# Grouping the attention score products on TensorE two rounds at a time, in a fused attention and MLP kernel

## The chip, the cores and the metric

The kernel runs on one core of a Trainium2 chip. The metric is the device time of one execution in microseconds: the median over three runs before the change is 751.19 us, and the change is judged by the same measurement.

## The reference

One input x of 2048 rows by 512 goes through two branches, which a gate mixes. Branch A is attention with 32 heads of 16 columns, where each row attends to itself and the 255 rows before it. Branch B is an MLP with 1792 hidden columns and a GELU.

```python
qkv = (x @ wqkv).reshape(B, S, 3, H, Dh).transpose(2, 0, 3, 1, 4)
q, k, v = qkv[0], qkv[1], qkv[2]
scores = einsum("bhqd,bhkd->bhqk", q, k) * Dh ** -0.5
mask = (i - j >= 0) & (i - j < 256)
o = einsum("bhqk,bhkd->bhqd", softmax(where(mask, scores, -1e9)), v)
a = o.transpose(0, 2, 1, 3).reshape(B, S, D) @ wo
b = gelu(x @ w1 + b1) @ w2 + b2
g = sigmoid((x * gate_w).sum(-1))
out = g * a + (1 - g) * b
```

## The kernel before

All dense products (x times wqkv, w1, w2, wo) are done with each operand split into a high and a low part, so one logical product is three matmuls of 128x512, on lines 108, 109 and 110 (`mm3`). One such step is called a dense step below; the Python generator `dense()` yields after each. It goes first through the query, key and value products (tiles `qk`, `v`), then through eight MLP passes (for each a stretch of seven tiles `u` with the GELU, and a stretch of four tiles `y`), and at last through the output product (tiles `a`).

Attention runs beside this. It works in eight groups of four heads, and each group in sixteen blocks of 128 rows, so there are 128 block steps. The scores are computed twice. The first time, `att_max` (a matmul on line 519 into a tile `sm`) puts 128x320 scores into PSUM, and VectorE reduces them to a maximum per row (line 524, tiles `jm` and `M`). The maxima of four blocks are turned round (`att_rows`, lines 536 to 546) and appended as rows to the queries. The second time, `att_exp` (a matmul on line 564 into a tile `st`) gives scores with the maximum already taken off, ScalarE writes their exponentials (line 586, tile `pt`), and GpSimd cuts the masked corners (line 580). After every fourth block, `att_pvs` multiplies 12 half blocks of exponentials with the values (line 608): many small matmuls into one bank of the `sm` ring and one of the `st` ring. ScalarE copies the one (line 629, tile `nd`), VectorE adds the other (line 632), and both banks are free again.

The PSUM rings are short: three buffers `sm`, three buffers `st`, two buffers `d` for the dense tiles. A product into `sm` can start when the product three places before it in that ring has been reduced; for `st`, when the third before it has been exponentiated. A bank that `att_pvs` takes counts as a place.

The order of instructions on each engine is fixed when the program is built. Python code issues the TensorE instructions in the order written, keeps a clock of estimated time (`tick`), and puts everything that follows a product on a heap with a delay (`after(ns, fn)`); what has come due is issued as the clock moves on. On the chip each engine executes its own list in order and waits for the others by semaphores.

The order around the change is set by the main loop, with `LEAD = 12`, `STEP = 2330`, `PVAT = 2` and `ORDER = 'mspf'`. Each block step u consists of four rounds i. A round issues one product of maxima (letter m, for the block 12 steps ahead), one product of exponentials (letter s), in round 2 the value products of the block before where they are due (letter p), and then a share of dense work (letter f). In the first twelve block steps there are only maxima, in the last twelve only exponentials.

```python
def fill(ns):
    owed[0] += ns
    while owed[0] > 0:
        c = next(run)          # one dense step; c is its estimate, 681
        ...
            owed[0] -= c
            tick(c)
```

A round owes 2330/4 = 582.5 of dense work and a dense step counts 3 x 227 = 681, so most rounds issue one dense step and about every seventh none.

Of the kernel before, what the change touches and what calls it, by code (L numbers as in the profile page):

```python
# [32 lines left out]
def gated_mix(ctx: ExitStack, tc: tile.TileContext, x, wqkv, wo, w1, b1, w2, b2, gate_w, out):  # L33
# [60 lines left out]
    for s in (0, 1):  # L94
        for k in (0, 1):
            v = own[64 * s:64 * s + 4].rearrange("r (p s) -> r s p", s=2)[:, s]
            nc.gpsimd.affine_select(out=v, in_=v, pattern=[[-2, 2]], compare_op=ALU.not_equal,
                                    fill=1.0, base=-k, channel_multiplier=1)
# [16 lines left out]
    def after(ns, fn, *args):  # L115
        now[1] += 1
        heapq.heappush(todo, (now[0] + ns, now[1], fn, args))
# [7 lines left out]
    def tick(ns):  # L125
        now[0] += ns
        while todo and todo[0][0] <= now[0]:
            step_todo()
# [331 lines left out]
    def load_ks(g_, c):  # L460


        ready(c, g_, 1)
        n = 2 * NB
        put_pairs([f32(ks[64 * s + 4:64 * s + 52, slot(g_, c)]) for s in range(2)], SK[c], g_)
# [16 lines left out]
    def load_kd(g_, c):  # L482
        for t in range(max(c - 1, 0), c + 1):
            ready(t, g_, 1)
            k0 = 0 if t == c else T - W
            at = W if t == c else 0
            src = heads(SK[t], g_)[:, :, :, :, k0:].rearrange("s d u a c -> (s d u) a c")
            nc.sync.dma_start(f32(kd[0:96, slot(g_, c), :, at:at + T - k0]), src)

    def load_qd(g_, c):  # L490
        ready(c, g_, 0)
        put_pairs([f32(qd[48 * s:48 * s + 48, slot(g_, c)]) for s in range(2)], SQ[c], g_)

    def load_qs(g_, c):
        ready(c, g_, 0)
        need(("v", NT - 2, NB - 1))
        for s in range(2):
            v = f32(qs[64 * s + 4:64 * s + 52, :, c * T:(c + 1) * T])
            nc.sync.dma_start(v, part(SQ[c], g_, s).rearrange("r (a c) -> r a c", a=2))

    def att_load_v(g_, c):
        need(*[("v", c, b) for b in range(NB)])
        vt = vbuf[:, c % 2]
        dst = vt[:, 0:NB * 68].rearrange("p (j c) -> p j c", c=34)
        nc.sync.dma_start(dst, SV[c].rearrange("p j s c -> p (j s) c")[:, :, 34 * g_:34 * g_ + 34])
        vts[g_, c] = vt

    def att_max(g_, b, i):

        if b % RB == 0 and (g_, b // RB) not in Ms:  # L510
            Ms[g_, b // RB] = sb.tile([128, 2 * RB, 2], F32, tag="M", bufs=2, name=f"M{g_}_{b}")
        M = Ms[g_, b // RB]
        hb, pr = divmod(i, 2)
        c, n = b // NB, slot(g_, b // NB)
        j = 2 * (b % NB) + hb
        w = min(64 * (2 * b + hb + 1), W + 64)
        k1 = 64 * (j + 1) + W
        p = ps.tile([128, 320], F32, tag="sm", bufs=3, name=f"sm{g_}_{b}_{i}")
        nc.tensor.matmul(p[:, :w], qd[0:96, n, pr, 128 * j:128 * (j + 1)], kd[0:96, n, pr, k1 - w:k1],  # L519
                         start=True, stop=True)  # L520
        junk = cs.tile([128, 320], BF16, tag="jm", bufs=1, name=f"jm{g_}_{b}_{i}")

        def red():
            nc.vector.tensor_tensor_reduce(junk[:, :w], p[:, :w], mask[:, 320 - w:320], 1.0, -3e38,  # L524
                                           ALU.add, ALU.max, M[:, 2 * (b % RB) + hb, pr:pr + 1])
            done.add(("max", g_, b, i))
        tick(w / 2.4 + 13)
        after(100, red)
# [310 lines left out]
    def load_y(t):  # L839

        need(*[("y", 1, t, b) for b in range(NB)])
        for i in range(NB // 2):
            if t < 2:
                v = f32(qd[:, t, i]).rearrange("p (j f) -> p j f", j=2)
            else:
                v = f32(kd[:, i, :, 0:T])
            nc.sync.dma_start(v, YB[t].rearrange("(i j p) f -> i p j f", j=2, p=128)[i])
            for j in range(2):
                ybs[t * NB + 2 * i + j] = v[:, j]
# [56 lines left out]
# [4 lines that stand above are left out]
            c = next(run)  # L910
            if c is None:
                owed[0] = -1e9
            else:
                owed[0] -= c
                tick(c)
# [7 lines left out]
    for u in range(-LEAD, NU):  # L923
        m = u + LEAD
        gm, bm = divmod(m, NKB)
        step = STEP if u >= 0 else STEP0
        for i in range(4):
            if i == 1 and m % NB == 0 and NB <= m < NU - NB:
                load_kd(*divmod(m // NB + 1, NT)), load_qd(*divmod(m // NB + 1, NT))
            for op in ORDER:  # L930
                if op == "s" and u >= 0:
                    att_exp(u // NKB, u % NKB, i)
                if op == "m" and m < NU:
                    att_max(gm, bm, i ^ XOR)
                if op == "p" and i == PVAT and u >= 1:
                    att_pvs(u - 1)
                if op == "f":
                    fill(step / 4 / ORDER.count("f"))
        if m < NU and bm % RB == RB - 1:
            after(900, att_rows, gm, bm // RB)  # L940
        if m % NB == QAT % NB and QAT <= m < QAT + NKB:
            load_qs(0, (m - QAT) // NB)
        if u % NB == 0 and NB <= u < NU - NB:
            load_ks(*divmod(u // NB + 1, NT))
        if u % NB == 2 and NB < u < NU - 3 * NB:
            load_qs(*divmod(u // NB + 3, NT))
        if u % NB == 0 and u >= 0:
            att_load_v(*divmod(u // NB, NT))
        if u - NU + NKB in (9, 11, 13):
            load_y((u % NKB - 9) // 2)  # L950
# [23 lines left out]
ORDER = 'mspf'  # L974
# [36 lines left out]
```

## Time and profile before

| | |
|---|---|
| three runs | 751.12, 751.19, 751.46 us; median 751.19 us |
| profiled execution | 752.58 us, of which 750.6 us are its span from the first to the last instruction |
| busy in the span | PE (TensorE) 98%, its weight loads 81%, DVE (VectorE) 69%, ACT (ScalarE) 57%, POOL (GpSimd) 50% |
| score products | 512 on line 519 (from 119.9 to 653.8 us), 512 on line 564 (the exponentials on ScalarE run from 161.7 to 699.6 us) |

The ends of matmuls are modelled, and matmuls overlap in the pipeline, so the cost of a matmul on TensorE is read as the distance from its start to the next start, not as its duration. "F" below is one dense step (lines 108, 109, 110), "m" a product on line 519, "s" one on line 564, "P" the value products on line 608.

### The profile page before, as it was taken

To read this page: it belongs to the slowest core of one execution; us is meant where nothing else is said; L and a number is where in the kernel's file an instruction comes from. 1 tells how busy PE (TensorE), PEld (TensorE's weight loads), DVE (VectorE), ACT (ScalarE), POOL (GpSimd) and SP (SyncE) were. 2 spreads that over 40 slices of the span, in tenths; PEclk is the share of its full clock that TensorE was granted. 3 is DMA by queue.
4 is the path that set the end of the run, shared out by engine and by line. 5 is a ranking of instruction groups with operands and counts; after the bars stand their busy time and mean duration, and the time that the engine had idled before them with its cause. 6 is when DMAs were issued, how large, how long until landed. Compare 5 with 4: busy or idle time off the path is not lost.

```text
span 750.6 us, 17969 instructions
## 1 busy us (share of the span) xinstructions
PE 733.8 (98%) x6129; PEld 605.3 (81%) x6129; DVE 519.6 (69%) x1567; ACT 430.9 (57%) x972; POOL 372.0 (50%) x846
## 2 busy tenths in 40 slices
PE   8999999998999999999999999999999999999998
PEld 6888888876788888888887877888888888878787
DVE  4532325789758867986898689868867886784552
ACT  4434522358547845864696478547845854785541
POOL 4200000339756765786577657757865875630000
PEclk9999999999999999999999999999999999999999
DMA  9889798998995687799576889996799898538783
GB/s 315 328 275 402 258 387 274 254 316 186 272 253 141 153 242 203 186 226 263 143 180 167 214 230 219 253 243 153 179 259 246 203 237 217 135 88 263 226 265 115
DMA packets 179258, 172.10 MB, mean 229 GB/s; under 512 B 56672, under 2 KB 122976, under 8 KB 179168
## 3 DMA queue, kind: packets, MB, share of 16 engines
q1 hardware_dynamic: 179168, 170.97, 81.0%
q8 instruction: 48, 0.79, 0.5%
q14 instruction: 42, 0.34, 0.2%
HBM read 108.53 MB, written 62.39 MB: 228 GB/s over the span
## 4 chain that ended last, share of the span: by engine, by line
PE 83%; DMA 6%; DVE 4%; ACT 2%; issue 2%; SPq 1%; POOL 0%; DVEq 0%; ACTq 0%; POOLq 0%
PE sm L519 9%; PE st L564 8%; PE y L108 7%; PE pv_sm L608 6%; PE y L110 6%; PE y L109 6%; PE u L108 5%; PE u L109 5%; PE u L110 5%; PE qk L110 4%; PE qk L108 4%; PE qk L109 4%; PE v L108 2%; PE a L108 2%; PE v L110 2%
## 5 line engine op out<-in xcount | busy, mean ns | idle before, releaser
L524 DVE CUSTOM_DVE_ANT_0 jm<-sm,mask 128x320 bf16<-128x320 f32 (+4 forms) x512 | 237.9, 465 | 83.4 <-PE sm L519 55.7
L580 POOL TENSOR_SCALAR_AFFINE_SELECT pt<-pt 64x256 f32<-64x256 f32 (+1 forms) x538 | 225.8, 440 | 118.6 <-ACT pt L586 108.2
L586 ACT ACTIVATE pt<-st 128x320 f32<-128x320 f32 (+4 forms) x512 | 207.1, 425 | 131.7 <-PE st L564 128.4
L519 PE MATMUL sm<-kd,qd 96*128 96x320 f32 (+4 forms) x512 | 156.3, 308 | 6.1 <-DVE M L524 3.8
L564 PE MATMUL st<-qs,ks 128*128 128x320 f32 (+4 forms) x512 | 155.7, 307 | 1.2 <-ACT pt L586 1.2
L546 POOL CAST qs<-tt 4x256 fp32r<-4x256 f32 x256 | 126.2, 493 | 42.4 <-DVE tt L539 31.4
L519 PEld LDWEIGHTS sm<-kd,qd 96*128 96x128 f32 x512 | 96.1, 188 | 34.3 <-DVE M L524 10.9
L564 PEld LDWEIGHTS st<-qs,ks 128*128 128x128 f32 x512 | 97.2, 190 | 21.5 <-ACT pt L586 2.3
L108 PE MATMUL y<-w,h 128*128 128x512 f32 x224 | 89.9, 401 | 0.0
L110 PE MATMUL y<-w,h 128*128 128x512 f32 x224 | 88.4, 395 | 0.3 <-DVE h L737 0.3
L109 PE MATMUL y<-w,h 128*128 128x512 f32 x224 | 88.2, 394 | 0.0
L108 PE MATMUL u<-mx,w 128*128 128x512 f32 x196 | 80.0, 408 | 0.0
L109 PE MATMUL u<-mx,w 128*128 128x512 f32 x196 | 77.3, 394 | 0.0
L110 PE MATMUL u<-mx,w 128*128 128x512 f32 x196 | 77.2, 394 | 0.0
L608 PE MATMUL pv_st<-pt,vbuf 64*32 64x320 f32 (+4 forms) x1408 | 73.2, 346 | 2.5 <-DVE pt L574 1.3
L608 PE MATMUL pv_sm<-pt,vbuf 64*32 64x320 f32 (+4 forms) x1408 | 74.1, 346 | 0.1
L608 PEld LDWEIGHTS pv_sm<-pt,vbuf 64*32 64x32 f32 x1408 | 51.1, 106 | 19.1 <-issue 2.3
L325 DVE TENSOR_TENSOR qke<-qk,qke 128x512 fp32r<-128x512 f32 x32 | 22.1, 690 | 47.4 <-ACT qke L322 39.3
L322 ACT ACTIVATE qke<-qk 128x512 fp32r<-128x512 f32 x32 | 19.1, 598 | 55.6 <-PE qk L110 32.3
L110 PEld LDWEIGHTS y<-w,h 128*128 128x128 f32 x224 | 42.1, 188 | 10.7 <-DVE h L737 1.2
L608 PEld LDWEIGHTS pv_st<-pt,vbuf 64*32 64x32 f32 x1408 | 46.0, 106 | 2.8 <-DVE pt L574 1.5
L338 POOL MEMSET vx<- 128x32 f32 x16 | 2.4, 156 | 89.2 <-DMA SQ<-qke 42.9
(148 smaller groups left out, 1334.4 us busy)
## 6 DMA issues: line engine op xcount, KB each, us to landing
kd<-SK SPq DMA_DIRECT2D x32, 384.0 KB
qs<-SQ SPq DMA_DIRECT2D x64, 192.0 KB
mx<-XT SPq DMA_DIRECT2D x24, 512.0 KB
SQ<-qke SPq DMA_DIRECT2D x16, 512.0 KB
SK<-qke SPq DMA_DIRECT2D x16, 512.0 KB
ND<-nd SPq DMA_DIRECT2D x32, 256.0 KB
raw_w<-in_B_w_dram SPq DMA_DIRECT2D x28, 256.0 KB
ks<-SK SPq DMA_DIRECT2D x32, 192.0 KB
```

Source lines behind the costliest of these rows:

```text
L108: nc.tensor.matmul(p, lh, rh, start=first, stop=False)
L109: nc.tensor.matmul(p, lh, rl, start=False, stop=False)
L110: nc.tensor.matmul(p, ll, rh, start=False, stop=last)
L322: nc.scalar.activation(e[:, h], p, AF.Copy)
L325: nc.vector.tensor_sub(e[:, 1 - h], p, f32(e[:, h]))
L519: nc.tensor.matmul(p[:, :w], qd[0:96, n, pr, 128 * j:128 * (j + 1)], kd[0:96, n, pr, k1 - w:k1], start=True, stop=True)
L524: nc.vector.tensor_tensor_reduce(junk[:, :w], p[:, :w], mask[:, 320 - w:320], 1.0, -3e38, ALU.add, ALU.max, M[:, 2 * (b % RB) + hb, pr:pr ...
L546: nc.gpsimd.tensor_copy(dst, src.unsqueeze(1).broadcast_to([4, 2, RB, 32]))
L564: nc.tensor.matmul(p[:, :w], ks[:, slot(g_, kb // NB), pr, at:at + 128], qs[:, pr, k0:k0 + w], start=True, stop=True)
L580: nc.gpsimd.affine_select(out=v, in_=v, pattern=[[0, v.shape[1]], [1 - 2 * e, 64]], compare_op=ALU.is_ge, fill=0.0, base=-e, channel_multi ...
L586: nc.scalar.activation(pt[:, hf, pr, :w], p[:, :w], AF.Exp, scale=SCALE)
L608: nc.tensor.matmul(pv[r // 64][32 * i:32 * i + 32, q - c * T:e - c * T], vts[g_, b // NB][r:r + 64, v:v + 32], rhs(r), start=start, stop=s ...
```

## The change

The loop over the four rounds now works on two rounds at a time. For rounds 0 and 1, and again for rounds 2 and 3, it issues the m, the s (and P, if due) of both rounds first, and then the two shares of dense work. So a row of m s F m s F becomes m s m s F F. Where a round owed no dense step, a pair has one F in place of two. In the first twelve block steps m F m F becomes m m F F, and in the last twelve s F s F becomes s s F F. The value products still follow the m and s of round 2, and now the m and s of round 3 follow them directly. The loads of `kd` and `qd` at `i == 1` are now issued after the dense work of rounds 0 and 1, not after that of round 0 alone. Nothing is added or removed.

```diff
         for i in range(4):
             if i == 1 and m % NB == 0 and NB <= m < NU - NB:
                 load_kd(*divmod(m // NB + 1, NT)), load_qd(*divmod(m // NB + 1, NT))
-            for op in ORDER:
+            if i % 2 == 0:
+                pair = (i, i + 1) if True else (i,)
+            elif len(pair) == 2:
+                continue
+            else:
+                pair = (i,)
+            for op, i in [(op, k) for k in pair for op in ORDER[:3]] + [("f", k) for k in pair]:
                 if op == "s" and u >= 0:
                     att_exp(u // NKB, u % NKB, i)
                 if op == "m" and m < NU:
@@
                 if op == "p" and i == PVAT and u >= 1:
                     att_pvs(u - 1)
                 if op == "f":
-                    fill(step / 4 / ORDER.count("f"))
+                    fill(step / 4)
```

On TensorE, at the end of the third set of value products (`pv_2`; its last matmul starts at 220.04 us in the profile), the order before is:

```order
L608 MATMUL pv_2_sm<-pt_6_2202,vbuf 32x128
L519 MATMUL sm_8_2_2659<-kd,qd 128x320
L564 MATMUL st_12_3_2663<-qs,ks 128x320
L108 MATMUL y_03_2530<-w_5_2001,h_5_2021 128x512
L109 MATMUL y_03_2530<-w_5_2001,h_5_2021 128x512
L110 MATMUL y_03_2530<-w_5_2001,h_5_2021 128x512
L519 MATMUL sm_9_1_2680<-kd,qd 128x320
L564 MATMUL st_13_0_2684<-qs,ks 128x320
L108 MATMUL y_03_2530<-w_6_2119,h_6_2144 128x512
L109 MATMUL y_03_2530<-w_6_2119,h_6_2144 128x512
L110 MATMUL y_03_2530<-w_6_2119,h_6_2144 128x512
L519 MATMUL sm_9_0_2693<-kd,qd 128x320
```

The same place on TensorE after the change (`sm_9_0` is the product of maxima for block 9, round 0, and so on; the last number is a buffer's):

```order
L608 MATMUL pv_2_sm<-pt_6_2202,vbuf 32x128
L519 MATMUL sm_8_2_2659<-kd,qd 128x320
L564 MATMUL st_12_3_2663<-qs,ks 128x320
L108 MATMUL y_03_2535<-w_5_2000,h_5_2032 128x512
L109 MATMUL y_03_2535<-w_5_2000,h_5_2032 128x512
L110 MATMUL y_03_2535<-w_5_2000,h_5_2032 128x512
L519 MATMUL sm_9_1_2680<-kd,qd 128x320
L564 MATMUL st_13_0_2684<-qs,ks 128x320
L519 MATMUL sm_9_0_2688<-kd,qd 128x320
L564 MATMUL st_13_1_2692<-qs,ks 128x320
L108 MATMUL y_03_2535<-w_6_2125,h_6_2152 128x512
L109 MATMUL y_03_2535<-w_6_2125,h_6_2152 128x512
```

`sm_9_0` takes the bank that `pv_2` gives back (the third place before it in the ring), and it now stands one dense step earlier behind the value products.

On VectorE, around the addition that frees the bank of the next set (`nd_3`), the order before is:

```order
L737 TENSOR_TENSOR h_0_3874<-x1h_0_3874_3882,h_0_3874 128x512
L650 RECIPROCAL den_0_3928<-den_0_3928 128x32
L731 SCALAR_TENSOR_TENSOR x1h_1_3948_3954<-sqh_1_3948_3955,x1h_1_3948_3954 128x512
L632 TENSOR_TENSOR nd_3_4044<-nd_3_4044,pv_3_sm 128x512
L524 ISA jm_12_2_4053,M_12_3939<-sm_12_2_4051,mask 128x320
L524 ISA M_12_3939 128x1
L524 ISA jm_13_1_4074,M_12_3939<-sm_13_1_4072,mask 128x320
```

and after the change it is:

```order
L737 TENSOR_TENSOR h_0_3878<-x1h_0_3878_3883,h_0_3878 128x512
L650 RECIPROCAL den_0_3928<-den_0_3928 128x32
L524 ISA jm_12_2_4047,M_12_3939<-sm_12_2_4045,mask 128x320
L524 ISA M_12_3939 128x1
L632 TENSOR_TENSOR nd_3_4044<-nd_3_4044,pv_3_sm 128x512
L731 SCALAR_TENSOR_TENSOR x1h_1_3955_3961<-sqh_1_3955_3962,x1h_1_3955_3961 128x512
L524 ISA jm_13_1_4074,M_12_3939<-sm_13_1_4072,mask 128x320
```

The reduction of the product that follows the value products has moved ahead of the addition on line 632, and a step of the GELU (line 731) has moved behind it.

## The prediction

> **What bounds the kernel now.** I read the page first, for the engine that is full.
>
> ```profile
> span 750.6 us, 17969 instructions
> PE 733.8 (98%) x6129; PEld 605.3 (81%) x6129; DVE 519.6 (69%) x1567; ACT 430.9 (57%) x972; POOL 372.0 (50%) x846
> PEclk9999999999999999999999999999999999999999
> ```
>
> TensorE is at work nearly all the time at full granted clock. The change adds and removes no matmul, so it can act in two ways only: the matmuls could follow each other more or less closely, and TensorE could wait more or less for a PSUM bank. For the second I looked at who holds up the products of maxima (the view of line 519), and who holds up VectorE (the view of waits).
>
> ```profile
> L519 PE MATMUL sm<-kd,qd x512: 193/311/418, 119.9 to 653.8; 96*128 96x320 f32 x150, 96*128 96x128 f32 x6, 96*128 96x64 f32 x5, 96*128 96x256 f32 x5
>   DVE M L524: 14.7, 32
>   DVE yo L811: 2.7, 2
>   DVE nd L632: 2.7, 4
> ```
>
> ```profile
> DVE nd L632 <- ACT nd L629: 23.2, 15, 3.0
> ```
>
> Of 512 products, 32 were held up by an earlier reduction, 14.7 us in all with their weight loads (which partly overlap other matmuls, so the loss is a little less), 2 by the end of a dense tile and 4 by the addition that frees the bank of the value products. Those are the waits to watch. Then the table of stretches, to see where they lie: busy times of PE, PEld, DVE, ACT and POOL in each.
>
> ```profile
> 170.00:180.00 10.00, 8.40 (x39) 5.93 (x38) 9.14 (x24) 8.59 (x20) 9.47 (x15) 1.00 0.68 157
> 180.00:190.00 10.00, 9.70 (x112) 7.82 (x111) 9.37 (x29) 8.86 (x20) 9.40 (x19) 1.00 1.08 274
> 300.00:320.00 20.00, 20.00 (x250) 16.53 (x249) 19.00 (x57) 16.04 (x35) 15.61 (x30) 1.00 0.77 191
> 340.00:360.00 20.00, 20.00 (x188) 16.86 (x187) 12.72 (x47) 8.89 (x21) 12.05 (x34) 1.00 0.89 254
> 380.00:400.00 20.00, 19.08 (x160) 15.88 (x159) 18.70 (x57) 17.36 (x39) 15.83 (x31) 1.00 0.81 181
> 440.00:450.00 10.00, 9.43 (x46) 7.28 (x46) 9.13 (x27) 8.33 (x19) 5.74 (x13) 1.00 0.88 208
> 450.00:460.00 10.00, 9.39 (x107) 7.07 (x105) 9.27 (x28) 8.92 (x19) 7.25 (x15) 1.00 0.97 222
> 460.00:470.00 10.00, 9.35 (x47) 7.47 (x46) 9.28 (x29) 8.20 (x20) 8.21 (x16) 1.00 0.88 219
> ```
>
> VectorE's mean of 69% hides two kinds of stage. In a `y` stage such as 340 to 360 it is busy 12.72 of 20 us and TensorE never waits. In a `u` stage, where the GELU steps come on top of the reductions, it is busy over nine tenths, and TensorE falls below full in six of the rows above (all but 300 to 320 and 340 to 360). There VectorE sets the pace, and how far TensorE may run ahead of it is a matter of the three `sm` banks.
>
> **The distance between matmuls.** Groups of four exist already, where a round owed no dense step. The timeline of TensorE shows one:
>
> ```profile
> 305.89 0.31 PE L519 MATMUL sm<-kd,qd 96*128 96x320 f32 x1
> 306.04 0.31 PE L564 MATMUL st<-qs,ks 128*128 128x320 f32 x1
> 306.19 0.32 PE L519 MATMUL sm<-kd,qd 96*128 96x320 f32 x1
> 306.34 0.31 PE L564 MATMUL st<-qs,ks 128*128 128x320 f32 x1
> 306.50 0.40 PE L108 MATMUL u<-mx,w 128*128 128x512 f32 x1
> ```
>
> Each score product takes 0.15 us (0.16 before the dense one), in a group of four as in a group of two, so regrouping costs TensorE nothing by itself. I take 0.0 us. Even 0.01 us for each of 256 groups would be 2.6 us in either direction, and I keep 1 us of that for the range.
>
> **The run-ahead.** A dense step takes 0.69 us, read from this place behind the value products `pv_2` (timeline of PE, ACT and DVE):
>
> ```profile
> 220.04 0.27 PE L608 MATMUL pv_sm<-pt,vbuf 64*32 64x128 f32 x1
> 220.24 0.42 PE L519 MATMUL sm<-kd,qd 96*128 96x320 f32 x1
> 220.40 0.60 ACT L629 ACTIVATE nd<-pv_st 128x512 f32<-128x512 f32 x1 [1.94 <-PE pv_sm L608]
> 220.49 0.31 PE L564 MATMUL st<-qs,ks 128*128 128x320 f32 x1
> 220.64 0.39 PE L108 MATMUL y<-w,h 128*128 128x512 f32 x1
> 220.69 0.49 DVE L524 CUSTOM_DVE_ANT_0 jm<-sm,mask 128x320 bf16<-128x320 f32 x1 [2.31 <-PE sm L519]
> 221.10 0.68 DVE L632 TENSOR_TENSOR nd<-nd,pv_sm 128x512 f32<-128x512 f32 x1
> 221.33 0.31 PE L519 MATMUL sm<-kd,qd 96*128 96x320 f32 x1
> 221.48 0.31 PE L564 MATMUL st<-qs,ks 128*128 128x320 f32 x1
> 221.63 0.39 PE L108 MATMUL y<-w,h 128*128 128x512 f32 x1
> 222.33 0.31 PE L519 MATMUL sm<-kd,qd 96*128 96x320 f32 x1
> ```
>
> The dense step runs from 220.64 to 221.33, 0.69 us, and a round with one lasts 0.99 to 1.00 us. A product of maxima reuses the bank of the third before it. Before, these two always lie three rounds apart: 3 x 0.99 = 2.97 us when every round has its dense step. After, it depends on the place in the pair. From the first m of a pair to the second m of the next pair lie two dense steps and six score products, 2 x 0.69 + 6 x 0.15 = 2.28 us; from the second m to the first m of the pair after the next, 3.66 us. The half that got more room gains nothing where there was enough. The half that got less is the one that counts: the reduction must now be over 0.69 us sooner. (Where a round owes no dense step, both figures are 0.69 us lower: 2.28 before, 1.59 after.)
>
> Where is a reduction later than 2.28 us? In the `u` stages. Two places from the timeline, each a product and what releases its bank; the first also with the product that waits for it:
>
> ```profile
> 173.48 0.34 PE L519 MATMUL sm<-kd,qd 96*128 96x320 f32 x1
> ...
> 176.75 0.48 DVE L524 CUSTOM_DVE_ANT_0 jm<-sm,mask 128x320 bf16<-128x320 f32 x1
> 177.16 0.08 DVE L524 DVE_READ_ACCUMULATOR2_ANT M<- 128x1 f32 x1
> 177.29 0.41 PE L519 MATMUL sm<-kd,qd 96*128 96x320 f32 x1 [0.65 <-DVE M L524]
> ...
> 447.45 0.31 PE L519 MATMUL sm<-kd,qd 96*128 96x320 f32 x1
> ...
> 449.44 0.49 DVE L524 CUSTOM_DVE_ANT_0 jm<-sm,mask 128x320 bf16<-128x320 f32 x1
> ```
>
> The product of 173.48 was reduced at 177.23, 3.75 us later. The product three places on would have been ready at 173.48 + 2.97 = 176.45 and waited until 177.29. The product of 447.45 was reduced at 449.93, 2.48 us later: no wait before, but 0.20 us beyond the new limit. So in stages where TensorE waits already, it arrives 0.69 us sooner at the same wait, and the backlog that it may build up is smaller by that. The loss comes once in each stretch, since afterwards VectorE sets the pace in both orders. I count one for each of the six rows in which PE is below full: 6 x 0.69 = 4.1 us. The lower bound is 0, if VectorE's order gets better by as much. The upper bound lets the shorter limit bite at every one of the 32 + 2 + 4 = 38 waits, one product in two being the tight one: 38 x 0.69 / 2 = 13.1 us.
>
> **The bank of the value products.** By the orders shown, the second m of the next pair takes this bank. Counted in the row of TensorE, after 7 of the 28 sets that have maxima behind them there is one dense step up to that m, after the others two. In the rows above, after the change: m at 220.24, s at 220.49, dense step 220.64 to 221.33, m at 221.33, s at 221.48, m due at 221.63. The addition on line 632 ends at 221.78, and a product follows its release by 0.05 us (177.24 to 177.29), so it starts at 221.83: 0.20 us lost. Before, the same product came at 222.33 and was safe. With two dense steps it comes 0.69 us later and is safe unless VectorE is behind. Seven times 0.20 is 1.4 us; two of the seven lie in `u` stages, where VectorE is later, and I add 0.45 us for each (two thirds of the addition's 0.68). Together 2.3 us, between 0 and 7 x 0.69 = 4.8 us.
>
> **What gets better.** The reduction of the m behind the value products moves ahead of the addition, while VectorE otherwise waits for ScalarE's copy: 23.2 us of waiting in 15 cases. This uses 0.48 + 0.08 = 0.56 us of idle time, but it is worth something only where VectorE is the bound: I count two sets in the slow stretches, 1.1 us gained, between 0 and 6 x 0.56 = 3.4 us. Exponentials have the same shorter distance on the `st` ring, but ScalarE is the lesser load in the rows above except near 450 to 460; I take 0 and leave this to the range. The loads of `kd` and `qd` start one half step later and are used four block steps later: 0.
>
> **The sum.** 0.0 + 4.1 + 2.3 - 1.1 = +5.3 us. The profiled execution, 752.6 us, would become 757.9; against the median of 751.2 this gives **756.5 us**.
>
> **Rivals.** *The waits go away (10%).* If the two reductions side by side and the earlier one behind the value products let VectorE run its list without holes, part of the 14.7 + 2.7 + 2.7 = 20.1 us would go; a third of it gives 751.2 - 6.7 = 744.5. It decides from the point where the holes filled outweigh 0.69 us a stretch. For it speak the 23.2 us of VectorE's waits, against it that VectorE is busy 9.1 to 9.4 of 10 us in those stretches and has few holes left.
>
> *Nothing moves (8%).* The rings suffice in the `y` stages, VectorE sets the pace in the `u` stages in either order, and only the seven sets cost: 751.2 + 1.4 - 1.1 = 751.5. Against it speaks that the limit of 2.28 us lies below lags that the trace shows.
>
> *The limit bites every time (13%).* With two dense steps in a row, VectorE runs dry during them and is overrun after them, so that the loss comes again in each pair: 751.2 + 13.1 + 2.3 = 766.6. Against it speaks that VectorE has three reductions queued when it is behind, 3 x 0.56 = 1.7 us of work, as long as the two dense steps.
>
> *The clock falls (1%).* In the stretches 170 to 190 and 380 to 400 TensorE has waits and a granted clock of 1.00 even at 8.40 of 10 us busy, so more of them should not change it. If it halved in the six waiting stretches, their PE time of 8.40 + 9.70 + 19.08 + 9.43 + 9.39 + 9.35 = 65 us would double, to 816 us. The Trainium skill, in "TensorE: Matmul & The Clock Gate", section "A second HAM failure mode: psum-queue depth-cycling", says that a kernel that cycles through PSUM banks can pause so often between matmul groups that the clock gate swings between half and full rate. By that rule this change would be the wrong direction; the trace, with short waits and 1.00 throughout, does not show it.
>
> **How the numbers follow.** The forecast, some microseconds slower, has 68%; its own range is 753 to 763. A measurement of this kernel can tell about 0.2%, 1.5 us, from no change. Faster by more than that is the first rival, 10%; within it the second, 8%; slower the rest, 82%. The range of 751.5 to 767 takes in the forecast, half of the second rival and nearly all of the third, and leaves out the first.
>
> **What would show it.** In the profile after, the waits of line 519 for M should grow from 32 cases to 40 or more, and those for nd from 4 to about 11. The stretches 170 to 190, 380 to 400 and 440 to 470 should show PE further below full, the `y` stages still full, and the score products should still start 0.15 us apart. The prediction is wrong if the waits shrink, if the products in a group of four spread to 0.19 us or more, or if TensorE waits in `y` stages beyond the seven places.

## The result, and the profile after

The kernel is slower by 3.0 us: 754.16 us (753.76 to 755.27 in six runs) against 751.15 us for the kernel before (749.35 to 751.54 in six runs), a ratio of 1.0040 with a 95% interval of 1.0026 to 1.0054. The forecast was +5.3 us, with a range that holds the result. The profiled execution has a span of 753.6 us, 3.0 more than before. The six executions of a kernel spread over 1.5 to 2.2 us here, and those of the kernel before over 4.9 to 7.2 us in the larger sets behind the experiments, so differences under one microsecond are read from many runs or not at all.

The page after, in the lines that answer to those of before:

```profile
span 753.6 us, 18000 instructions
PE 734.8 (98%) x6129; PEld 605.2 (80%) x6129; DVE 524.3 (70%) x1567; ACT 420.5 (56%) x972; POOL 372.7 (49%) x846
PEclk9999999999999999999999999999999999999999
```

The view of line 519 after, and then the one line of the view of line 564 that names ScalarE as the releaser, before and after:

```profile
  DVE M L524: 21.4, 43
  issue: 4.0, 20
...
  DVE nd L632: 0.2, 1
```

```profile
  ACT pt L586: 3.5, 8
```

```profile
  ACT pt L586: 7.1, 12
```

The products of maxima wait 6.7 us more for earlier reductions, in 43 cases and not 32. The products of exponentials wait 3.6 us more for ScalarE. Two waits are gone: 2.7 us for the end of a dense tile (line 811), and nearly all of the 2.7 us for the bank of the value products. These sums hold the weight loads' waits too, so they exceed what TensorE lost; the span says 3.0 us. The cases are counted twice in part as well: the 32 are 22 weight loads and 10 matmuls of the same products, the 43 are 33 and 10. So 22 products of maxima were held up by a reduction before, and 33 after. The line "issue" stands for 20 weight loads with 0.2 us each in which the profile shows nothing waited for.

Which products are held up shows the mechanism best. The rounds are issued in pairs, so each product of maxima is the first or the second m of its pair, and the trace keeps their order. Before, 11 of the 22 held-up products were ones that the change makes second; after, 31 of the 33 are. The second m is the one whose distance to the third place before it became shorter.

The same stretches as before:

```profile
170.00:180.00 10.00, 8.53 (x42) 6.77 (x40) 9.10 (x24) 8.46 (x20) 9.51 (x17) 1.00 0.52 130
180.00:190.00 10.00, 9.63 (x111) 7.95 (x112) 9.29 (x30) 8.55 (x19) 7.70 (x15) 1.00 1.08 265
300.00:320.00 20.00, 19.89 (x227) 16.36 (x211) 19.00 (x58) 15.58 (x34) 17.05 (x33) 1.00 0.83 193
340.00:360.00 20.00, 20.00 (x188) 16.84 (x187) 12.79 (x46) 7.99 (x21) 11.53 (x33) 1.00 0.88 249
380.00:400.00 20.00, 18.07 (x154) 14.76 (x153) 18.21 (x55) 16.67 (x38) 15.88 (x31) 1.00 0.72 173
440.00:450.00 10.00, 9.28 (x42) 6.86 (x41) 8.84 (x26) 8.27 (x20) 7.18 (x14) 1.00 0.84 204
450.00:460.00 10.00, 9.38 (x110) 7.53 (x109) 9.57 (x29) 8.79 (x19) 7.47 (x16) 1.00 0.63 184
460.00:470.00 10.00, 8.79 (x42) 6.90 (x41) 8.93 (x27) 7.80 (x18) 8.11 (x16) 1.00 1.11 233
```

The `y` stage at 340 is full as before. In the six stretches where PE was below full, its busy time falls from 65.4 to 63.7 us. The granted clock stays at 1.00 in all of them.

Where along the program the time goes can be read from the starts of the 32 sets of value products, which stand at the same place of the work in both orders. A table of some of them, worked out from the two traces (after minus before, in us):

| set that started before at | 182.5 | 199.5 | 217.9 | 367.6 | 402.6 | 473.3 | 523.3 | 573.3 | 606.0 | 656.2 | 671.0 | 699.5 |
|---|---|---|---|---|---|---|---|---|---|---|---|---|
| after | -0.1 | -0.1 | -1.4 | -1.5 | -0.6 | +0.5 | +1.0 | +1.3 | +2.6 | +2.3 | +3.7 | +3.4 |

So the change first wins 1.3 us between 199 and 218 (the wait for line 811 that is gone), stands nearly still up to 367, and then loses 4.9 us in five steps of about 1 us, each in a `u` stage or at the start of the `y` stage behind it.

### The profile page after: what moved, and what is told of

Read it like the earlier page. It is cut to its first block, busy times and chain, and to the rows that moved or that the text cites. A ratio compares the mean times of both kernels' runs of the same rounds, so it can differ in the third digit from the quotient of the medians.

```text
span 753.6 us, 18000 instructions
## 1 busy us (share of the span) xinstructions
PE 734.8 (98%) x6129; PEld 605.2 (80%) x6129; DVE 524.3 (70%) x1567; ACT 420.5 (56%) x972; POOL 372.7 (49%) x846
## 4 chain that ended last, share of the span: by engine, by line
PE 78%; DMA 7%; DVE 7%; ACT 3%; issue 3%; SPq 1%; POOL 0%; DVEq 0%; ACTq 0%; POOLq 0%
PE sm L519 9%; PE st L564 7%; PE pv_sm L608 6%; PE y L108 6%; PE y L109 6%; PE y L110 6%; PE u L108 4%; PE u L109 4%; PE u L110 4%; PE qk L110 4%; PE qk L108 4%; PE qk L109 4%; DVE jm L524 2%; DMA qs<-SQ 2%; PE v L108 2%
## 5 line engine op out<-in xcount | busy, mean ns | idle before, releaser
L586 ACT ACTIVATE pt<-st 128x320 f32<-128x320 f32 (+4 forms) x512 | 194.4, 423 | 139.6 <-PE st L564 137.2
L546 POOL CAST qs<-tt 4x256 fp32r<-4x256 f32 x256 | 128.5, 502 | 69.9 <-DVE tt L539 59.8
L519 PE MATMUL sm<-kd,qd 96*128 96x320 f32 (+4 forms) x512 | 154.6, 317 | 7.6 <-DVE M L524 5.9
L564 PE MATMUL st<-qs,ks 128*128 128x320 f32 (+4 forms) x512 | 153.1, 309 | 2.6 <-ACT pt L586 2.4
L719 ACT ACTIVATE x1h<-u,b1c 128x512 f32<-128x512 f32 x56 | 38.7, 691 | 13.2 <-DVE h L737 6.5
```

The costliest lines, as they stand in the source:

```text
L546: nc.gpsimd.tensor_copy(dst, src.unsqueeze(1).broadcast_to([4, 2, RB, 32]))
L564: nc.tensor.matmul(p[:, :w], ks[:, slot(g_, kb // NB), pr, at:at + 128], qs[:, pr, k0:k0 + w], start=True, stop=True)
L586: nc.scalar.activation(pt[:, hf, pr, :w], p[:, :w], AF.Exp, scale=SCALE)
L719: nc.scalar.activation(x1, p, AF.Identity, bias=b1c[:, f:f + 1])
```

## The experiments

Theory A was that of the prediction: the products of maxima have the shorter run-ahead on the `sm` banks, which VectorE empties. Theory B: the same shortening on the `st` banks, which ScalarE empties. Theory C: two dense steps in a row after four score products, which starve VectorE and ScalarE and then flood them. Ratios are to the kernel before on the same chip in the same session, with 95% intervals. The diffs are shortened to the lines that matter; `j` and `k` are the two rounds of a pair, and the loop runs over `ops`.

### One kind of product in pairs, the other evenly spaced

```diff
-            for op, i in [(op, k) for k in pair for op in ORDER[:3]] + [("f", k) for k in pair]:
+            # m in pairs
+            ops = [("m", j), ("s", j), ("p", j), ("m", k), ("f", j), ("s", k), ("p", k), ("f", k)]
+            # s in pairs
+            ops = [("m", j), ("s", j), ("p", j), ("s", k), ("f", j), ("m", k), ("p", k), ("f", k)]
```

For the paired maxima:

> Only the products of maxima stand in pairs (m s m F s F); the products of exponentials stay evenly spaced, about as before. Theory A (the loss is the shorter run-ahead on the three sm banks, which VectorE empties): nearly the whole loss stays, 753 to 755 us against 751.2 before, and the waits of line 519 for M stay near 21 us. Theory B (the loss is the same shortening on the st banks, which ScalarE empties): 750.5 to 752 us, and the waits of line 564 fall back from 7.1 to near 3.5 us. Theory C (it is the two dense steps in a row, which starve VectorE and ScalarE and then flood them): little of the loss is left, since here one dense step stands between any two groups, 750.5 to 752 us.

Measured: 750.66 us, ratio 0.9991 (0.9975 to 1.0008). For the paired exponentials:

> Only the products of exponentials stand in pairs (m s s F m F); the products of maxima stay evenly spaced. Theory A (sm banks, VectorE): 750 to 752.3 us, waits of line 519 for M near the 14.7 us of before. Theory B (st banks, ScalarE): 753 to 755 us, waits of line 564 near 7 us. Theory C (two dense steps in a row): 750.5 to 752 us, as for the kernel with paired maxima.

Measured: 752.63 us, ratio 1.0015 (0.9997 to 1.0034). The releasers of line 519 with paired maxima, and of line 564 with paired exponentials:

```profile
  DVE M L524: 18.1, 31
...
  DVE nd L632: 0.4, 1
```

```profile
  ACT pt L586: 6.8, 16
```

In each kernel the waits of the shortened ring are longer in sum than before (18.1 against 14.7 us, 6.8 against 3.5 us), as A and B say. But the time does not follow: with the maxima alone in pairs nothing is lost, so theory A in its simple form falls. All 21 products of maxima that are held up by a reduction there are second ones, as in the change. It may be that the longer waits cost something there and that the gains of the change, which this kernel has too (no wait for line 811, nearly none for nd), cancel it; no run here separates the two. With the exponentials alone, 752.63 us lies outside all three forecasts, and the loss of 1.1 us can be told neither from none nor from a good part of the change's 3.0 us. What is left is theory C, that both rings have to be short together, or that each ring costs a part.

### Both rings short, with a dense step between the pairs

```diff
+            ops = [("m", j), ("m", k), ("f", j), ("s", j), ("p", j), ("s", k), ("p", k), ("f", k)]
```

> Both kinds stand in pairs, but with a dense step between them (m m F s s F), so that both rings have the short distance of 2.28 us as in the change, and no two dense steps are neighbours. Theory of the rings (both rings short at once is what costs): 753 to 755 us against 751.2 before, as for the change. Theory C (two dense steps in a row after four score products): 750 to 752 us.

Measured: 754.13 us, ratio 1.0031 (1.0016 to 1.0047). The waits of line 519:

```profile
  DVE M L524: 26.8, 43
```

The whole loss is back, although no two dense steps are neighbours where both kinds of product are issued. Theory C falls: two dense steps in a row are not needed for the loss. The shortest distance is a little less here than the 2.28 us of the change: by the same sum, five score products and two dense steps, 2 x 0.69 + 5 x 0.15 = 2.13 us, on both rings (and on the `st` ring with paired exponentials).

### Four rounds in one group

```diff
+            if i:
+                continue
+            ops = [(op, k) for k in range(4) for op in ORDER[:3]] + [("f", k) for k in range(4)]
```

> All four rounds of a block step are grouped: eight score products, then three or four dense steps. The fourth m of a group then stands 0.90 us behind the first, whose bank it needs, and the fourth s likewise. Theories of the rings: each block step waits 0.1 us or more in the y stages and 1 us or more in the u stages, 770 to 800 us, with waits at line 519 in more than 100 cases. A theory by which the run-ahead does not matter and only the order on VectorE does: under 758 us.

Measured: 802.59 us, ratio 1.0663 (1.062 to 1.0706). The releasers of lines 519 and 564:

```profile
  DVE M L524: 72.2, 102
```

```profile
  ACT pt L586: 14.4, 24
```

The same mechanism in a larger dose. The fourth product of a group needs the bank of the first, which started only about 0.90 us before it, and 57 of the 59 products of maxima that are held up by a reduction are the fourth of their group. The loss of 51 us goes with 72.2 us of waits for reductions (weight loads included). The run-ahead that three banks allow is what grouping uses up. A part of the loss has another source: the granted clock, which falls behind some of the long waits here (last section). Its mean of 0.992 over 804.7 us stands for about 6 us, as an estimate.

### Which stages

```diff
-                pair = (i, i + 1) if True else (i,)
+                pair = (i, i + 1) if phase[0] == "y" else (i,)     # or: != "y"
```

> Rounds are paired as in the change, but only while the dense work is of the y tiles; in the u tiles and all else the order is that of before. Theory A: VectorE is not behind in the y stages, so nothing is lost: 749.5 to 752 us. A theory by which grouping costs something at every place, in whatever stage: about half of the loss, 752.3 to 753.2 us.

Measured: 751.62 us, ratio 1.0002 (0.9986 to 1.0018).

> Rounds are paired as in the change everywhere but in the y stages. Theory A: the whole loss is here, in the u stages and the stages with maxima alone or exponentials alone: 753.3 to 756 us. A theory by which grouping costs something at every place: 752.3 to 753.2 us.

Measured: 752.51 us, ratio 1.0014 (0.9999 to 1.0029). Pairing in the `y` stages alone costs nothing that can be measured. Pairing everywhere else gives 752.51 us, less than the 753.3 us that theory A had as its least, and in the range of the other theory, which the first of these two kernels does not bear out. The two effects add up to 1.6 parts in a thousand, where the change has 4.0; the intervals are wide enough for that gap. A part of the loss may arise only where a paired `y` stage follows a paired `u` stage. The traces lean that way: beside dense steps of `y`, 9 products of maxima are held up by a reduction in the change, 4 before, and 2 where the `y` stages are not paired. This is not settled.

### The last twelve block steps

```diff
-                pair = (i, i + 1) if True else (i,)
+                pair = (i, i + 1) if u < NU - LEAD else (i,)
```

> The change, except that the last twelve block steps, with exponentials alone, keep the order of before (s F s F, not s s F F). If the loss of 1.4 us that the profile after shows between the value products at 656 and at 671 us comes from the paired exponentials: 752.3 to 753.5 us. If it moves elsewhere or was chance: 753.7 to 755 us.

Measured: 754.82 us, ratio 1.0046 (1.0031 to 1.0061). The step of 1.4 us between the sets at 656 and 671 shrinks to 0.3 us in this trace, but the time as a whole is no better. So the exponentials alone at the end are not where the loss is made. All twelve executions of this kernel had a mean granted clock of 1.000, so the clock is not where it is made either.

### VectorE or ScalarE relieved

One GELU step of one engine is left out of both orders:

```diff
         def f2():
-            nc.vector.scalar_tensor_tensor(sq, sq, GC, x1, op0=ALU.add, op1=ALU.mult)
+            pass
```

> The order of before, with one of VectorE's three GELU steps (line 725, 0.69 us each, 56 of them) left out, so the GELU's result is another. Partner of the next kernel. VectorE is then hardly behind in the u stages: all theories 744 to 750 us, the waits of line 519 for M well under the 14.7 us of before.

> The order of the change with the same VectorE step left out. Read against its partner. Theory A (sm banks, VectorE): the loss of 3.0 us shrinks to -1 to +1 us, since VectorE is no longer behind. Theory B (st banks, ScalarE): the loss stays at 2 to 4 us, and the waits of line 564 for ScalarE stay about twice the partner's. Theory C (two dense steps in a row after four score products): about 1 to 2 us.

Measured: 742.92 us (0.9899, 0.9873 to 0.9924) and 743.55 us (0.9904, 0.9885 to 0.9923).

```diff
         def f1():
-            nc.scalar.activation(sq, p, AF.Square, bias=b1c[:, f:f + 1])
+            pass
         def f2():
-            nc.vector.scalar_tensor_tensor(sq, sq, GC, x1, op0=ALU.add, op1=ALU.mult)
+            nc.vector.scalar_tensor_tensor(sq, x1, GC, x1, op0=ALU.add, op1=ALU.mult)
```

> The order of before, with one of ScalarE's GELU steps (line 722, the square, about 0.69 us each, 56 of them) left out, so the GELU's result is another; VectorE's next step reads the plain value. Partner of the next kernel. All theories: 747 to 751 us.

> The order of the change with the same ScalarE step left out. Read against its partner. Theory B (st banks, ScalarE): the loss of 3.0 us shrinks to -1 to +1 us. Theory A (sm banks, VectorE): it stays at 2 to 4 us. Theory C: about 1 to 2 us.

Measured: 748.18 us (0.9966, 0.9951 to 0.9980) and 750.13 us (0.9992, 0.9979 to 1.0006). The waits of line 519 for reductions in these four kernels, in the order of the text:

```profile
  DVE M L524: 3.9, 8
```

```profile
  DVE M L524: 7.3, 13
```

```profile
  DVE M L524: 12.9, 30
```

```profile
  DVE M L524: 18.5, 33
```

With less ScalarE work, the waits of line 564 for ScalarE are small in both orders, before and after the change:

```profile
  ACT pt L586: 2.1, 2
```

```profile
  ACT pt L586: 2.9, 7
```

Less VectorE work brings 7 to 8 us to the order of before, and the change then costs 0.6 us, within the scatter of these six runs each. Less ScalarE work brings 2 to 3 us, and the change still costs 2.0 us, although ScalarE's waits are nearly gone. This agrees with VectorE's lateness in the `u` stages as the condition for the loss, and speaks against theory B. It also fits badly with the idea that both rings have to be late together. By the intervals of the ratios, each of the two differences, 0.6 and 2.0 us, is uncertain by about 2.4 and 1.5 us, so they are not far enough apart to call it settled.

### A version that might beat both

Since a lighter VectorE was worth so much, three of seven GELU tiles had their last step done by GpSimd, in the order of before, with nothing left out:

```diff
-            nc.vector.tensor_sub(h[:, 1], x1, f32(h[:, 0]))
+            eng = nc.gpsimd if f % HF in (0, 2, 4) else nc.vector
+            eng.tensor_sub(h[:, 1], x1, f32(h[:, 0]))
```

> The order of before; of the seven GELU tiles of each u stage, three have their last step (line 737, 0.69 us on VectorE) done by GpSimd, where such a subtraction takes 1.29 us. Nothing is left out. If VectorE's lateness is what TensorE waits for, 24 of 56 steps should bring 24/56 of the 7.2 us that 56 steps brought when they were left out, about 3 us: 747 to 749.5 us. If GpSimd, 70 to 83% busy in the u stages, falls behind with the masked corners and the rows of maxima instead: 750 to 755 us.

Measured: 758.46 us, ratio 1.0082 (1.0053 to 1.0111), slower, and beyond both forecasts. The group of the moved step on GpSimd, then the view of line 719 (the first GELU step on ScalarE) in this kernel:

```profile
L738 POOL TENSOR_TENSOR h<-x1h,h 128x512 fp32r<-128x512 f32 x24 | 34.0, 1415 | 7.3 <-issue 4.5 <-ACT h L734 0.6 <-POOL qs L546 0.5
```

```profile
  POOL h L738: 9.2, 7
```

and the releaser of line 564 in it:

```profile
  ACT pt L586: 11.3, 12
```

The step takes 1.4 us on GpSimd, and it stands in line behind GpSimd's masks. Until it is done, one of the two `x1` buffers is held; ScalarE waits 9.2 us in seven cases for one, with the exponentials queued behind. The products of exponentials then wait for ScalarE, 11.3 us against 3.5. Behind one such wait, which kept TensorE from its next matmul from 177.3 to 179.1 us, the granted clock is 0.50 from 182 to 184 us; this dip is worth about 1.7 us of the loss, as an estimate. No version here that does all the work beats both kernels; the order of before and the one with paired maxima alone cannot be told apart.

## Why the prediction was right, and where it was not

**What bounds the kernel, and the distance between matmuls: right.** In the profile after a group of four has starts 0.15 us apart, as read from the groups of before:

```profile
219.97 0.31 PE L519 MATMUL sm<-kd,qd 96*128 96x320 f32 x1
220.12 0.31 PE L564 MATMUL st<-qs,ks 128*128 128x320 f32 x1
220.27 0.31 PE L519 MATMUL sm<-kd,qd 96*128 96x320 f32 x1
220.42 0.31 PE L564 MATMUL st<-qs,ks 128*128 128x320 f32 x1
220.57 0.39 PE L108 MATMUL y<-w,h 128*128 128x512 f32 x1
```

**The run-ahead, 4.1 us: the mechanism was right, its place too narrow.** The waits of line 519 for reductions grew to 43 cases (forecast: 40 or more), which are 33 products and not 22; 31 of the 33 are the half that got less room, as the prediction says; and the group of four rounds shows the mechanism plainly. (The prediction read the 32 and the 38 as products; they were 22 and 25, and its upper bound of 13.1 us would have been 8.6.) But the prediction put the whole of it on the `sm` ring and took zero for the `st` ring ("ScalarE is the lesser load"). The runs show no loss with the short `sm` ring alone (0.9991), 1.0015 with the short `st` ring alone, and the loss with both (1.0040, 1.0031, 1.0046 in three kernels). The two alone add up to 1.0006, and the intervals just reach from there to the 1.0040; so how the two work together, and whether `st` counts at all, stays open. The places were not those counted either: the stretches 170 to 190 lost nothing by the table of sets, and two of the six rows did not fall (8.40 to 8.53 of 10 us, 9.39 to 9.38), while the five `u` stages from 367 on lost about 1 us each instead of 0.69 a row.

**The bank of the value products, 2.3 us: wrong.** The step that failed is "the second m of the next pair takes this bank". The timeline after, at the set that the prediction used, with the rows of the addition and of that m:

```profile
218.68 0.27 PE L608 MATMUL pv_sm<-pt,vbuf 64*32 64x128 f32 x1
218.88 0.42 PE L519 MATMUL sm<-kd,qd 96*128 96x320 f32 x1
219.75 0.08 DVE L524 DVE_READ_ACCUMULATOR2_ANT M<- 128x1 f32 x1
219.75 0.68 DVE L632 TENSOR_TENSOR nd<-nd,pv_sm 128x512 f32<-128x512 f32 x1
220.27 0.31 PE L519 MATMUL sm<-kd,qd 96*128 96x320 f32 x1
```

The second m of the next pair starts at 220.27, while the addition still runs until 220.43. So it is not in that bank. The buffers are handed out in the order in which the program gives them back, not strictly in turn. The reduction of the m behind the value products is now listed ahead of the addition, so its bank comes back first and goes to this m, and the value products' bank goes to the m after it. In the built program this is so for all 28 sets. (The m in question then takes a bank used only two places before it; this is so with the maxima alone in pairs too, where nothing is lost, and hardly at all with a dense step between the pairs, where the whole loss is there, so it is not the cause.) The same holds already for 5 of the 28 sets before, this one among them, so the sentence on it in the description of the change is wrong as well. Waits for nd fell from 4 cases to 1, where 11 were forecast: this term was at least 2.3 us too high.

**What gets better, 1.1 us: the sign was right.** VectorE's waits for ScalarE's copy fell from 23.2 us in 15 cases to these:

```profile
DVE nd L632 <- ACT nd L629: 4.3, 4, 3.5
```

What this brought in time was not measured by itself. The 1.3 us gained around 206 us, where the wait for line 811 went away, were not foreseen.

**The sum.** Without the failed term the working would have given 4.1 - 1.1 = 3.0 us, which is what was measured; since the 4.1 were put on one ring alone and on other stretches than those that lost, this is luck and no proof of the rest. The rival in which the waits go away had the smaller half: 2.7 us for line 811 and 2.5 us for nd went, against 6.7 and 3.6 us that came. The rival in which nothing moves (751.5) lies outside the interval of the result. The rival in which the limit bites every time failed: 11 more products were held up, not one in every pair. The rival in which the clock falls failed for the change (1.00 in all eight stretches); its argument that more waits should not change the clock holds for short waits only, as the last section shows.

## What to carry to other kernels

Before products are grouped on a full engine, work out for each PSUM ring the distance in time from a product to the one that reuses its bank, at the tightest place of the new order; the mean is no help. A ring that loses run-ahead need not cost anything by itself, so check all rings that get shorter at once, and look at the stages where the emptying engine has little room left (over nine tenths busy in the `u` rows here), whatever its mean. Which buffer comes next is to be read from the built program: the pool may hand out what comes back first.

## What the runs showed of the hardware that was not expected

A product that had to wait for its bank delays the one behind it. From the timeline after:

```profile
398.43 0.31 PE L519 MATMUL sm<-kd,qd 96*128 96x320 f32 x1
398.57 0.30 PE L564 MATMUL st<-qs,ks 128*128 128x320 f32 x1
...
399.88 0.19 PEld L519 LDWEIGHTS sm<-kd,qd 96*128 96x128 f32 x1 [1.27 <-DVE M L524]
399.89 0.42 PE L519 MATMUL sm<-kd,qd 96*128 96x320 f32 x1 [1.01 <-DVE M L524]
400.14 0.31 PE L564 MATMUL st<-qs,ks 128*128 128x320 f32 x1
```

Without a wait the next product starts 0.14 to 0.15 us later, after a wait 0.25 us later (399.89 to 400.14). Over the whole trace, the median is 0.25 us for the 32 held-up products with a product of exponentials directly behind them, and 0.15 us for the others. The weights of the waiting product are loaded only after the wait as well (its load starts at 399.88), which may be why. So each of the 11 further held-up products costs about 0.1 us beside its own wait, as an estimate.

A long wait for a bank can be followed by a slower clock. In the kernel with four rounds in one group, TensorE starts no matmul from 173.71 to 177.50 us, and then the granted clock (the third figure from the end) halves for about three microseconds:

```profile
176.00:177.00 1.00, 0.00 (x0) 0.00 (x0) 1.00 (x3) 1.00 (x4) 0.49 (x1) 1.00 0.95 190
179.00:180.00 1.00, 1.00 (x4) 0.71 (x3) 1.00 (x4) 0.06 (x1) 0.95 (x3) 0.50 0.01 2
182.00:183.00 1.00, 1.00 (x8) 0.95 (x6) 0.52 (x1) 0.71 (x2) 0.91 (x2) 1.00 0.00 0
```

The matmuls of a dense step start 0.43 us apart there, and 0.23 us before. The clock halves at three more places in that kernel, and once in the profile of the kernel with paired `y` stages, behind a pause of 1.75 us. In the kernels before and after the change the longest pause while the score products are issued is 1.15 us, and the clock stays at 1.00. No limit follows from these few places.
